# A written TensorE order of dense blocks in a decode kernel with all its gradients

## The chip, the cores and the metric

The kernel runs on one core of one Trainium2 chip. The metric is the device time of one execution in microseconds (us). Every time below is the median of several executions, with the lowest and highest beside it where they matter. An execution that came out over 1.5% above the fastest of its kernel is called slow and left out of ratios. A ratio is the mean time of one kernel's fast runs over the mean time of the other kernel's fast runs in the same rounds on the same chip, so it is not quite the ratio of the medians quoted. A median takes in the slow executions too, so differences are given of medians and, where it matters, of the means of the fast runs. The batches ran on different chips. The fast runs of the kernel before have means of 566 to 571 us in them, so a difference between batches is sure to some 5 us only.

## The reference, cut to what matters

```python
# B=2, Sq=1, D=576, Hq=32, Hkv=16, Sk=4096, Dh=128, F=4608, all bf16
def _fwd_reference(A_x, A_k_cache, A_v_cache, A_wq, A_wo, B_x, B_w_gate, B_w_up, B_w_down):
    x = A_x
    xn = _layernorm(x)
    # A: q = xn @ wq; scores against k_cache; softmax; times v_cache; @ wo   (decode: one token)
    # B: (xn @ w_gate) * (xn @ w_up) @ w_down
    return x + _A_ref(xn, ...) + _B_ref(xn, ...)

def reference(..., grad_out):
    _out, _vjp = jax.vjp(_f, A_x, A_k_cache, A_v_cache, A_wq, A_wo, B_w_gate, B_w_up, B_w_down)
    return (_out, *_vjp(grad_out))
```

So the kernel reads both caches and all weights once (92.48 MB) and writes gradients of the same size (92.48 MB). The gradients of the caches and of the weights are outer products: TensorE makes them in PSUM, ScalarE and VectorE copy them to SBUF ("evacuate"), and DMA stores them.

## The kernel before

The work goes in 16 iterations, one for two K/V heads of one batch row. An iteration has eight "half heads". For each, VectorE transposes half of a head into `X`, and TensorE makes 16 score matmuls from it:

```python
    def ps_sc(): return ps.tile([P, P], FP32, tag="sc", bufs=2, name="ps_sc")      # scores
    def ps_o():  return ps.tile([P, 2, 512], FP32, tag="o", bufs=2, name="ps_o")   # outer products: two buffers

    def head_scores(n, t, x, s_ps, half):
        X = xtile([P, NCH, 64], "X")                         # 3 buffers
        t32(view(pairs(X[:]...)), view(pairs(n[:]...)))      # VectorE transpose
        for e in range(2):
            be = 2 * half + e
            for c8 in range(8):
                nc.tensor.matmul(s_ps[:], lhsT=view(W[t][:], ...), rhs=view(X[:], ...), ...)
```

The gradient of a K or V head leaves in units. Each unit takes one `ps_o` buffer, four matmuls in two row quadrants, and one copy:

```python
        def unit(A, cp):
            def f():
                if cp == 0:
                    m["st"] = stile([P, 2, 2, 8, Dh], "so")          # store buffer
                o = ps_o()
                for k in range(2):
                    for aa in range(2):
                        a = 2 * A + aa
                        nc.tensor.matmul(view(o[:], ...), lhsT=rows[32 * a:32 * a + 32, 2 * cp + k, :],
                                         rhs=bd[32 * a:32 * a + 32, :], start=True, stop=True)
                evac(view(m["st"][:], ...), o[:]..., 1024)
                if cp == 3:
                    ...                                              # two DMA stores
```

The weights' gradients have units of the same kind. Their store buffers (`stw`, `std`, `stq`, `sto`) share one pool of two:

```python
    def swtile(shape, name):
        return sb.tile(list(shape), BF16, tag="sw", bufs=2, name=name)

        def outer_o(A, h2, k):      # output projection: one store buffer per A, filled by four units
            def f():
                if h2 == 0 and k == 0:
                    m["so"] = swtile([P, 4, D], "sto")
                ...
```

One thing the text of the kernel does not show: the order in which TensorE gets its instructions is not that of the text. A scheduler of the framework chooses it when the program is built, from what is ready in its own estimate, so score blocks, outer units, softmax steps and weight pieces are laid between one another in small pieces.

Of the kernel before, what the change touches and what calls it, by code (L numbers as in the profile page):

```python
# [23 lines left out]
def kernel(  # L24
# [55 lines left out]
    def ps_o():  # L80
        return ps.tile([P, 2, 512], FP32, tag="o", bufs=2, name="ps_o")

# [177 lines left out]
    def dxn(Wm, Wt, weight, pos, koff, kstep):  # L260


        for half in range(2):
            dp = ps_m([P, 160])
            X = xtile([P, 9, FS // 2], "Xw")
            t32(view(pairs(X[:].rearrange("p c n -> p (c n)")), 0, P, 0, [[1, 9 * P]]),
                view(pairs(weight[:].rearrange("p c n -> p (c n)")), 0, P, P * half, [[2 * P, 9], [1, P]]))
            dve(1.4)
            for r in range(4):
                for gq in range(4):  # L270
                    q, s = 2 * half + gq // 2, 4 * (gq % 2) + r
                    nc.tensor.matmul(  # L272
                        dp[32 * gq:32 * gq + 32, 0:P], lhsT=view(Wm[:], 0, P, 8 * pos(q, s), [[1, 32]]),
                        rhs=view(X[:], 0, P, koff(s) * 256 + (2 * (q % 2) + (s // 2) % 2) * 64 + s % 2,
                                 [[kstep * 256, 4], [2, 32]]),
                        start=(r == 0), stop=(r == 3))
            for r in range(2):
                for gq in range(4):
                    q, s = 2 * half + gq // 2, 2 * (gq % 2) + r
                    nc.tensor.matmul(  # L280
                        dp[32 * gq:32 * gq + 32, P:160], lhsT=view(Wt[:], 0, P, 8 * (4 * q + s), [[1, 32]]),
                        rhs=view(X[:], 0, P, 8 * 256 + (2 * (q % 2) + s // 2) * 64 + s % 2, [[2, 32]]),
                        start=(r == 0), stop=(r == 1))
            nc.vector.tensor_add(accx[:], accx[:], dp[:])
            dve(0.35)


    def mlp_units(i):
# [62 lines left out]
        def back():  # L351
            dxn(*m["W"], m["wgu"], lambda q, s: q * 8 + s, lambda s: (s // 4) * 4, 1)

        def outer_gu(w, A):
            def f():
                hb = m["hb"]
                if A == 0:
                    m["st"] = swtile([P, 4, FS], "stw")
                st = m["st"]
                o = ps_o()  # L360
                for dc in range(4):
                    for aa in range(2):
                        a = 2 * A + aa
                        nc.tensor.matmul(o[:, aa, dc * P:(dc + 1) * P],  # L364
                                         lhsT=xnr[32 * a:32 * a + 32, dc * P:(dc + 1) * P],
                                         rhs=hb[32 * a:32 * a + 32, 1 + w, :], start=True, stop=True)
                evac(view(st[:], 0, P, 256 * A, [[P, 2], [FS, 4], [1, P]]),
                     o[:].rearrange("p a (d f) -> p a d f", d=4), 1024)
                if A == 1:
                    out = (out_6, out_7)[w]  # L370
                    nc.gpsimd.dma_start(out[0:512, f0:f0 + FS].rearrange("(c p) n -> p c n", p=P), st[:])  # L371
            return f

        def outer_tail():
            hb = m["hb"]
            st = tailtile("stt")
            for A in range(2):
                o = ps_o()
                for w in range(2):
                    for aa in range(2):  # L380
                        a = 2 * A + aa
                        nc.tensor.matmul(o[64 * w:64 * w + 64, aa, 0:P], lhsT=xnr[32 * a:32 * a + 32, 512:576],
                                         rhs=hb[32 * a:32 * a + 32, 1 + w, :], start=True, stop=True)
                evac(st[:, 256 * A:256 * A + 256].rearrange("p (a f) -> p a f", a=2), o[:, :, 0:P], 256)
            for w, out in enumerate((out_6, out_7)):
                nc.gpsimd.dma_start(out[512:576, f0:f0 + FS], st[64 * w:64 * w + 64])

        def outer_down(A, k):
            def f():
                hb = m["hb"]  # L390
                if A == 0 and k == 0:
                    m["sd"] = swtile([P, FC, D], "std")
                st = m["sd"]
                o = ps_o()
                for aa in range(2):
                    a = 2 * A + aa
                    nc.tensor.matmul(o[:, aa, 0:HD2], lhsT=hb[32 * a:32 * a + 32, 0, :],  # L397
                                     rhs=dyr[32 * a:32 * a + 32, k * HD2:(k + 1) * HD2], start=True, stop=True)
                evac(st[:, 2 * A:2 * A + 2, k * HD2:(k + 1) * HD2], o[:, :, 0:HD2], D)
                if A == 1 and k == 1:  # L400
# [3 lines left out]
        return [[loads], [gate_up, down], [grads, back], [outer_down(0, 0), outer_down(0, 1)], [outer_down(1, 0), outer_down(1, 1)],  # L404
                [outer_gu(0, 0), outer_gu(0, 1)], [outer_gu(1, 0), outer_gu(1, 1)], [outer_tail]]
# [14 lines left out]
    def group_front(g, wq, wo):  # L420
        qd = sb.tile([P, 3, GH, 2], BF16, tag="qd", bufs=2, name="qd")
        qp = ps_m([P, GH, 2])
        for h in range(GH):
            for dc in range(5):
                if dc < 4:
                    l, r = wq[:, 2 * dc + h // 4, (h % 4) * P:(h % 4 + 1) * P], xs[:, dc, 0:2]
                else:
                    l, r = wq[:, 8, (h % 4) * P:(h % 4 + 1) * P], xs[:, 4 + h // 4, 0:2]
                nc.tensor.matmul(qp[:, h, :], lhsT=l, rhs=r, start=(dc == 0), stop=(dc == 4))
        nc.vector.tensor_copy(qd[:, 0], qp[:])  # L430
        nc.vector.tensor_scalar(qd[:, 2], qd[:, 0], SCALE, None, op0=ALU.mult)

        do_ps = ps_m([P, GH * 32])
        for half in range(2):
            Xo = xtile([P, GH // 2, D], "Xo")
            t32(pairs(Xo[:].rearrange("p c n -> p (c n)")),
                pairs(wo[:, 4 * half:4 * half + 4].rearrange("p c n -> p (c n)")))
            for k in range(NB):
                for e in range(2):
                    nc.tensor.matmul(  # L440
                        do_ps[:, P * half:P * half + P], lhsT=Wdy[:, k, e, :],
                        rhs=view(Xo[:], 0, P, 64 * k + e, [[D, 4], [2, 32]]),
                        start=(k == 0 and e == 0), stop=(k == NB - 1 and e == 1),
                    )
        dof = sb.tile([P, GH, 32], FP32, tag="dof", bufs=1, name="dof")
        t32(dof[:].rearrange("p c n -> p (c n)"), do_ps[:])
        nc.vector.tensor_copy(qd[:, 1], dof[:, :, 0:2])


        rp = ps_m([P, 2, 4, GH * 2])  # L450
        for t in range(2):
            for be in range(4):
                nc.tensor.matmul(rp[:, t, be, :], lhsT=sel[:, be].rearrange("p a i -> p (a i)"),
                                 rhs=qd[:, t].rearrange("p h b -> p (h b)"), start=True, stop=True)
        rep = sb.tile([P, 2, 4, GH * 2], BF16, tag="rep", bufs=2, name="rep")
        nc.vector.tensor_copy(rep[:], rp[:])
        dve(2.6 + 1.2)
        return dict(g=g, wq=wq, wo=wo, qd=qd, rep=rep, oT=oTs[g % 2])
# [50 lines left out]
    def contract(rowsT, heads):  # L509
# [13 lines left out]
        o_sb = sb.tile([P, Dh], FP32, tag="o_sb", bufs=1, name="o_sb")  # L523
        nc.scalar.copy(o_sb[:], o_ps[:])
        act(0.3)
        t_ps = ps_m([P, 4])
# [11 lines left out]
    def outer_units(rows, bd, b, l0, oview):  # L538
        m = {}

        def unit(A, cp):
            def f():
                if cp == 0:
                    m["st"] = stile([P, 2, 2, 8, Dh], "so")
                o = ps_o()
                for k in range(2):
                    for aa in range(2):
                        a = 2 * A + aa
                        nc.tensor.matmul(view(o[:], 0, P, 512 * aa + P * k, [[256, 2], [1, P]]),  # L549
                                         lhsT=rows[32 * a:32 * a + 32, 2 * cp + k, :],  # L550
                                         rhs=bd[32 * a:32 * a + 32, :], start=True, stop=True)
                evac(view(m["st"][:], 0, P, 2 * cp * Dh, [[8 * Dh, 4], [1, 2 * Dh]]),
                     o[:].rearrange("p a (x c) -> p (a x) c", x=2), 1024)
                if cp == 3:
                    for aa in range(2):
                        nc.gpsimd.dma_start(oview[b, 2 * A + aa, :, l0:l0 + 2],  # L556
                                            m["st"][:, aa].rearrange("p x c d -> p x (c d)"))
            return f
        return [unit(A, cp) for A in range(2) for cp in range(4)]

    def softmax(s_ps):
        mx = small("mx")
        nc.vector.reduce_max(mx[:], s_ps[:], axis=AX.X)
        mT = ps_m([1, P])
        nc.tensor.transpose(mT[:], mx[:], identf[:])
        m4 = small("m4", (1, 4))
# [307 lines left out]
```

## Time and profile before

| | before |
|---|---|
| median of 3 runs | 571.89 us (568.31 to 573.84) |
| profiled span, mean TensorE clock | 561.8 us, 0.802 |
| TensorE busy | 472.1 us, 84% of the span |
| transfers | 186.13 MB, 329 GB/s over the span |

The page and the waits that carry the argument are shown and read in the prediction. The timeline of TensorE has the columns: start us, us, engine, line, operation, output and inputs, shapes, count. The timeline of TensorE before the change has the columns: start us, us, engine, line, operation, output and inputs, shapes, count; in brackets the idle time just before and what ended it.

```profile
123.80 1.08 PE L503 MATMUL ps_sc<-X,W 128*128 128x128 bf16 x16
124.82 0.61 PE L549 MATMUL ps_o<-bd,dsm 32*128 32x256 bf16 x8
125.36 1.09 PE L503 MATMUL ps_sc<-X,W 128*128 128x128 bf16 x16
126.38 0.39 PE L549 MATMUL ps_o<-bd,dsm 32*128 32x256 bf16 x4
126.70 0.18 PE L340 MATMUL ps_m<-gT,selA 128*128 128x16 bf16 x1
127.23 0.39 PE L549 MATMUL ps_o<-bd,dsm 32*128 32x256 bf16 x4 [0.34 <-ACT so L93]
```

At 126.38 one half of an outer unit (4 matmuls) is issued; the next half must wait until ScalarE has emptied a `ps_o` buffer. A weight-gradient matmul (L340) is laid into that time, and 0.34 us of it stay idle.

### The profile page before, as it was taken

To read this page: it belongs to the slowest core of one execution; us is meant where nothing else is said; L and a number is where in the kernel's file an instruction comes from. 1 tells how busy PE (TensorE), PEld (TensorE's weight loads), DVE (VectorE), ACT (ScalarE), POOL (GpSimd) and SP (SyncE) were. 2 spreads that over 40 slices of the span, in tenths; PEclk is the share of its full clock that TensorE was granted. 3 is DMA by queue.
4 is the path that set the end of the run, shared out by engine and by line. 5 is a ranking of instruction groups with operands and counts; after the bars stand their busy time and mean duration, and the time that the engine had idled before them with its cause. 6 is when DMAs were issued, how large, how long until landed. Compare 5 with 4: busy or idle time off the path is not lost. (4 is left out here: it accounts for less than half of the span.)

```text
span 561.8 us, 18035 instructions
## 1 busy us (share of the span) xinstructions
PE 472.1 (84%) x7897; PEld 336.5 (60%) x7897; DVE 369.6 (66%) x637; ACT 343.6 (61%) x473; POOL 193.3 (34%) x404
## 2 busy tenths in 40 slices
PE   2688859998989799999888973999898999888842
PEld 1576637676766465676677752666676666666511
DVE  8696836747656545738577672685787567788336
ACT  1146856857666264657667662686767559778631
POOL 5222443422432233333423441263433324433231
PEclk9899987857885655558888995697999569999656
DMA  8996999999699599689997897799999979985471
GB/s 259 407 395 225 418 407 383 339 369 365 189 412 404 199 304 410 229 305 395 360 398 270 342 418 310 263 404 415 363 399 381 420 275 385 394 347 219 158 270 49
DMA packets 53927, 186.13 MB, mean 331 GB/s; under 512 B 5164, under 2 KB 20152, under 8 KB 45656
## 3 DMA queue, kind: packets, MB, share of 16 engines
q1 hardware_dynamic: 28392, 92.49, 44.1%
q0 software_dynamic: 25456, 92.48, 42.1%
q8 instruction: 62, 1.02, 0.7%
q14 instruction: 17, 0.14, 0.1%
HBM read 92.48 MB, written 92.48 MB: 329 GB/s over the span
## 5 line engine op out<-in xcount | busy, mean ns | idle before, releaser
L93 ACT CAST so<-ps_o 128x1024 bf16<-128x1024 f32 x240 | 231.9, 1023 | 93.9 <-PE ps_o L549 90.1
L503 PE MATMUL ps_sc<-X,W 128*128 128x128 bf16 x2048 | 185.8, 240 | 2.5 <-DVE X L102 2.4
L102 DVE STREAM_TRANSPOSE X<-kv 128x1024 f32<-128x1024 f32 x128 | 157.5, 1233 | 33.6 <-PE ps_sc L503 27.7
L503 PEld LDWEIGHTS <-W 128*128 128x128 bf16 x2048 | 144.0, 107 | 34.6 <-issue 28.7
L556 POOL DMA_DIRECT2D out_dram<-so x128 | 91.4, 716 | 169.7 <-ACT so L93 74.0
L549 PE MATMUL ps_o<-bd,prm 32*128 32x256 bf16 x512 | 52.9, 304 | 10.5 <-ACT stq L93 4.7
L549 PE MATMUL ps_o<-bd,dsm 32*128 32x256 bf16 x512 | 54.8, 302 | 6.8 <-ACT so L93 4.4
L518 PE MATMUL ps_m<-kv,rowT 128*32 128x128 bf16 x2048 | 56.3, 251 | 1.0 <-issue 0.9
L518 PEld LDWEIGHTS <-rowT 128*32 128x32 bf16 x2048 | 38.4, 110 | 17.2 <-issue 13.8
L93 ACT CAST stw<-ps_o 128x1024 bf16<-128x1024 f32 x32 | 31.4, 1023 | 15.6 <-PE ps_o L364 8.8
L467 POOL COPY W<-rep 32x16 bf16<-32x16 bf16 x128 | 30.7, 240 | 20.6 <-PE ps_sc L503 13.7
L549 PEld LDWEIGHTS <-prm 32*128 32x128 bf16 x512 | 21.4, 98 | 22.6 <-issue 11.1
L549 PEld LDWEIGHTS <-dsm 32*128 32x128 bf16 x512 | 21.3, 98 | 19.8 <-issue 10.8
L93 ACT CAST std<-ps_o 128x576 bf16<-128x576 f32 x36 | 23.0, 648 | 12.9 <-PE ps_o L397 12.6
L474 POOL COPY dM<-qd 128x128 bf16<-128x128 bf16 x32 | 9.1, 289 | 61.7 <-PE ps_m L480 38.2
L93 ACT CAST stq<-ps_o 128x1024 bf16<-128x1024 f32 x10 | 9.9, 1013 | 28.3 <-DMA out_dram<-sto 26.1
L102 DVE STREAM_TRANSPOSE Xw<-wgu 128x1152 f32<-128x1152 f32 x18 | 24.5, 1362 | 3.3 <-PE ps_sc L503 3.3
L90 DVE CAST so<-ps_o 128x1024 bf16<-128x1024 f32 x16 | 19.3, 1208 | 11.1 <-PE ps_o L549 10.3
L93 ACT CAST sto<-ps_o 128x576 bf16<-128x576 f32 x30 | 18.8, 641 | 12.5 <-PE ps_o L684 12.3
L722 DVE TENSOR_SCALAR oT<-ps_m 128x4 bf16<-128x4 f32 x16 | 2.7, 170 | 35.4 <-PE ps_m L527 35.4
L371 POOL DMA_DIRECT2D out_dram<-stw x18 | 13.6, 753 | 23.0 <-ACT stw L93 11.5
L533 DVE TENSOR_TENSOR dsm<-ds,maskc 128x1024 bf16<-128x1024 bf16 x16 | 19.0, 1186 | 0.0
(178 smaller groups left out, 586.5 us busy)
## 6 DMA issues: line engine op xcount, KB each, us to landing
out_dram<-so POOLq DMA_DIRECT2D x128, 512.0 KB, 8.9
kv<-in_A_k_cache_dram SPq DMA_DIRECT2D x32, 1024.0 KB, 10.3
kv<-in_A_v_cache_dram SPq DMA_DIRECT2D x32, 1024.0 KB, 10.3
out_dram<-stw POOLq DMA_DIRECT2D x18, 512.0 KB, 9.1
wd<-in_B_w_down_dram SPq DMA_DIRECT2D x9, 576.0 KB, 9.5
out_dram<-std POOLq DMA_DIRECT2D x9, 576.0 KB, 6.9
wo<-in_A_wo_dram SPq DMA_DIRECT2D x4, 1152.0 KB, 13.6
wgu<-in_B_w_gate_dram SPq DMA_DIRECT2D x9, 512.0 KB, 11.7
```

The lines of the kernel that those rows point to most:

```text
L90: nc.vector.tensor_copy(out=out, in_=in_)
L93: nc.scalar.copy(out, in_)
L102: nc.vector.transpose(out, in_)
L371: nc.gpsimd.dma_start(out[0:512, f0:f0 + FS].rearrange("(c p) n -> p c n", p=P), st[:])
L467: nc.gpsimd.tensor_copy(view(W[t][:], 32 * a, 32, 28 + 32 * a, [[2 * WW, 4], [WW + 2, 2], [1, 2]]), view(st["rep"][:], 32 * a, 32, t * 4 * ...
L474: nc.gpsimd.tensor_copy(view(dM[:], 0, P, t * 2 * P, [[P + 2, 2], [4, 32], [1, 2]]), view(st["qd"][:], 0, P, (2 if t == 0 else 1) * GH * 2 ...
L503: nc.tensor.matmul(s_ps[:], lhsT=view(W[t][:], 0, P, (be * 2 + x) * WW + 28 - 4 * c8, [[1, P]]), rhs=view(X[:], 0, P, c8 * 64 + e, [[8 * 6 ...
L518: nc.tensor.matmul(o_ps[32 * cg:32 * cg + 32, :], lhsT=view(rowsT[:], 0, P, c4 * 32 + 4 * c8, [[1, 32]]), rhs=head[:, 8 * c4 + c8, :], sta ...
L533: nc.vector.tensor_tensor(m[:], view(rows[:], 0, P, 0, [[0, 8], [1, P]]), view(maskc[:], 0, P, 0, [[1, 8], [0, P]]), ALU.mult)
L549: nc.tensor.matmul(view(o[:], 0, P, 512 * aa + P * k, [[256, 2], [1, P]]), lhsT=rows[32 * a:32 * a + 32, 2 * cp + k, :], rhs=bd[32 * a:32 ...
L556: nc.gpsimd.dma_start(oview[b, 2 * A + aa, :, l0:l0 + 2], m["st"][:, aa].rearrange("p x c d -> p x (c d)"))
L722: nc.vector.tensor_scalar(st["oT"][:, 1, 4 * s:4 * s + 4, b], t_ps[:], SCALE, None, op0=ALU.mult)
```

## The change

The intent is to cut the switches between kinds of matmul: a switch is a pair of neighbours on TensorE that use the array in different tile shapes, and the prediction reads its price from the trace (some 93 ns each at full clock, 135 at half). TensorE's order is fixed to that of the text, and the text is laid out anew so that each half head is: one block of 16 scores, one K/V outer unit of four row quadrants (two `ps_o` buffers), one link of the chain (softmax, contraction, projection), about one weight piece.

```diff
+    ctx.enter_context(tc.manual_schedule(engines={mybir.EngineType.PE}))
...
-        def unit(A, cp):
+        def unit(cp):
             def f():
                 if cp == 0:
-                    m["st"] = stile([P, 2, 2, 8, Dh], "so")
-                o = ps_o()
+                    m["st"] = [stile([P, 2, 2, 8, Dh], "so") for _ in range(2)]
+                o = [ps_o(), ps_o()]
                 for k in range(2):
-                    for aa in range(2):
-                        a = 2 * A + aa
-                        nc.tensor.matmul(view(o[:], ...), ...)
-                evac(view(m["st"][:], ...), o[:]..., 1024)
+                    for a in range(4):
+                        nc.tensor.matmul(view(o[a // 2][:], ...), ...)
+                for A in range(2):
+                    evac(view(m["st"][A][:], ...), o[A][:]..., 1024)
...                                                       # the weights' units in the same way
-        def outer_o(A, h2, k):
+        def outer_o(h2, k):
...
+                if h2 == 0 and k == 0:
+                    m["so"] = [stq([P, 4, D], "sto") for _ in range(2)]     # both store buffers at once
...
+    for n in range(NIT + 1):
+        ...
+        for j in range(8):
+            head_scores(heads[x], t, x, cur[("s_ps", "dp_ps")[t]], half)    # 16 scores
+            more()                                                          # one K/V outer unit
+            if prev:
+                ...                                  # j = 0..3: contraction, selection of the iteration before
+            if live:
+                if 4 <= j < 7:
+                    soft[j - 4]()                    # one step of the softmax
+                ...
+                other(-(-len(side) // (12 - j)))     # about one weight piece
```

The arithmetic and the bytes stay the same.

## The prediction

> **What bounds the kernel now.** I read the page's header and its slices first, then TensorE's rows by form, the table of windows, the waits of each engine, and last the chain that ended last. A "slot" below is a half head: one transpose of keys or values into X on VectorE and 16 score matmuls. There are 128 of them (16 iterations of 8), so 562 us are 4.4 us a slot.
>
> ```profile
> PE 472.1 (84%) x7897; PEld 336.5 (60%) x7897; DVE 369.6 (66%) x637; ACT 343.6 (61%) x473; POOL 193.3 (34%) x404
> PEclk9899987857885655558888995697999569999656
> DMA  8996999999699599689997897799999979985471
> HBM read 92.48 MB, written 92.48 MB: 329 GB/s over the span
> ```
>
> TensorE is the busiest, but look at the two rows of digits: where the granted clock falls to 5 or 6, the transfers fall to 5 to 7 tenths, and where the clock is 9 they are at 9. The same from the windows (columns: busy us and instructions of each engine, granted clock, DMA share, GB/s):
>
> ```profile
> 200.00:240.00 40.00, 38.76 (x514) 25.32 (x513) 22.21 (x38) 24.11 (x32) 12.40 (x25) 0.54 0.84 307
> 400.00:440.00 40.00, 36.20 (x752) 27.46 (x751) 28.85 (x50) 28.87 (x38) 14.75 (x35) 0.97 0.98 380
> 460.00:500.00 40.00, 36.52 (x644) 25.51 (x644) 31.84 (x49) 32.61 (x44) 18.20 (x40) 1.00 0.99 387
> 520.00:562.00 42.00, 21.02 (x284) 10.63 (x276) 18.61 (x33) 15.74 (x20) 10.29 (x16) 0.58 0.43 157
> ```
>
> At 200 to 240 TensorE is busy 97% of the time and issues 514 matmuls; at 400 to 440 it issues 752. With a half clock TensorE is the bound; with a full one the kernel moves 380 to 387 GB/s and the DMA engines are full. The waits agree that it is not loads that hold anything up: no entry has VectorE waiting for a K or V load. The evacuations wait for TensorE:
>
> ```profile
> ACT so L93 <- PE ps_o L549: 90.1, 79, 4.0
> ACT stq L93 <- DMA out_dram<-sto: 26.1, 4, 9.9
> DVE X L102 <- PE ps_sc L503: 27.7, 31, 2.9
> PEld L503 <- issue: 28.7, 113, 0.7
> PE ps_o L549 <- ACT so L93: 7.8, 27, 0.5
> ```
>
> ScalarE waits 90 us for outer products, TensorE only 8 us for ScalarE. The 28.7 us of "issue" ahead of score weights, 113 times, are the price of coming back to scores from another kind of matmul. A stretch at half clock shows it, and a dense block at full clock beside it:
>
> ```profile
> 200.63 0.61 PE L549 MATMUL ps_o<-bd,prm 32*128 32x256 bf16 x4
> 201.17 0.29 PE L503 MATMUL ps_sc<-X,W 128*128 128x128 bf16 x1
> 201.39 0.40 PE L549 MATMUL ps_o<-bd,prm 32*128 32x256 bf16 x2
> 505.53 1.08 PE L503 MATMUL ps_sc<-X,W 128*128 128x128 bf16 x16
> ```
>
> [...] From the start times of neighbouring matmuls at full clock: score to score 57 ns (median), score to a 32-row outer product 150 ns, outer product to score 200 ns where its own 256 columns would need about 107. So some 93 ns a switch; at half clock (107, 241, 350 ns) some 135. [...] The trace's clock records are 0.5 or 1.0 only, in multiples of 3.41 us. I weighed each matmul of a window with its columns times its share of the 128x128 array (4 concurrent 32-row tiles count as one): whether this exceeds 0.34 of what a full clock could stream tells the next window's clock in 151 of 157 cases. 93 windows had a full clock, 65 a half one. [...] the trace has 3 to 6 ns between two quadrants. [...]
>
> **The change part by part.** The program built from each version (its order of instructions, no times) has the same 7813 matmuls and nearly the same ScalarE and VectorE work: 239 of 256 K/V evacuations on ScalarE against 240. What differs:
>
> 1. TensorE's order. Score runs go from 253 (mean 8.1) to 128 of exactly 16; contractions from 89 runs to 32 of 64; K/V outer products from 198 runs (105 of them of 4) to 125 nearly all of 8. Mode switches fall from 736 to 446. 290 x 0.093 = 27 us at full clock, 290 x 0.135 = 39 us at half.
> 2. An outer unit uses four row quadrants, not two. 8 matmuls of 256 columns then need two streams of 107 ns, not four. Their seven gaps cost 5+5+5+107+5+5+5 = 137 ns, against 7 x 39 in the mean of before: 128 x 0.136 = 17 us, at half clock 128 x 0.243 = 31 us.
> 3. Adding all start-to-start gaps by kind of neighbours over both orders: before 347 us at full clock and 585 at half; after 305 and 518, less item 2 288 and 487. Before spent 0.396 of its time at half clock, so without waits it would need 1/(0.604/347 + 0.396/585) = 412 us; 562 - 412 = 150 us are waits, of whatever kind. The new order at the same clock: 344 us.
> 4. The clock. Array work is 207 us (columns times share, all matmuls). Over 562 us this is 0.37, hardly above 0.34: hence the flapping, and the stretch at 199 to 247 us that stays at half. [...] In the new order, run without waits at half clock, it is 207/487 = 0.43: it should recover. At 505 us the mean is 0.41. Each slot also has its 16 score matmuls (16 x 53 = 0.85 us of array work), which evens it out. I expect a mean of about 0.90, not 1.0.
> 5. PSUM. A unit now takes both ps_o buffers. TensorE may start the next one only as the two evacuations end. Chain of before, near the end, where this already happens:
>
> ```profile
> 534.31 1.02 ACT so L93
> 535.33 0.04 issue
> 535.37 0.43 PE ps_o L684 x2
> 535.81 0.02 issue
> 535.83 0.65 ACT sto L93
> ```
>
> ScalarE is idle 0.50 us for each such turn. 201 units (128 of K/V, 73 of weights) x 0.5 = 100 us, on 344 us of ScalarE work: 444 us if every turn were exposed. This costs, but stays below item 6.
> 6. Transfers. 186.13 MB unchanged; at the 387 GB/s of a full-clock stretch 481 us. The start (0 to 20 us at 300 GB/s) loses some 5 us. The end now moves 157 GB/s x 42 us = 6.6 MB, 17 us' worth, so it loses 25. The last group's stores get buffers of the large pool and the last layer norm is laid between them: I take 18 lost instead of 25, a guess.
>
> Sum: TensorE 344 + 150 of waits = 494 us if clock and waits stay; transfers 481 + 5 + 18 = 504. The larger stands: a span of 504 us, 506 with the 1.8 us by which the timed run (563.56) exceeded its span (561.8). That is 12% below 571.89. The three timed runs of before are 5 to 10 us over the profiled one, so before is uneven by itself.
>
> **The rivals.** First, a rigid order waits where the old one filled in. In the old order a score block could be interrupted by whatever was ready; now one late X tile, one late small matmul of the softmax or a late store buffer stops everything behind it. For it: the 26.1 us of stq waiting for a store, up to 9.9 us at a time, and TensorE idle 9.4 us at 344 us because of it; the new output-projection piece takes both small store buffers at once. Against: chain links are spread one to a slot, a slot (4 us) being longer than any step of them. With 60 us more of waits: 565 us, the same as before. Second, the ps_o turn of item 5 becomes the bound in weight-heavy iterations: 16 K/V and some 24 weight evacuations, 20 turns at 0.5 us, some 43 us against some 41 us of transfers there. Worth 10 to 20 us: 515 to 525. Third, the clock goes to 1.0 and stores flow evenly: 186.13 MB at the 415 GB/s of the best slices is 449 us; with start and end 475 to 480. Fourth, stores: K/V output tiles are now allocated and sent in pairs, 2 MB at a time, and have four slots to land (16 us) where they had six. The median landing is 8.9 us; with full queues this can stall ScalarE; 5 to 15 us.
>
> **Range and chances.** Third rival alone gives 478, second and fourth together 540: this is my range for 8 in 10. Within 2% of before (560 to 583) needs the first rival in full, slower more than that. Since the gaps by kind show 68 us of TensorE time removed in any clock, and no work is added: faster 0.88, same 0.08, slower 0.04.
>
> **What would show it.** Score groups in runs of 16; "issue" ahead of score weights about halved; TensorE busy well below 84% of a smaller span, or below 400 us; mean clock 0.88 or more; slices with 9 tenths DMA through the middle; ScalarE's 90 us wait for outer products at 50 to 100, and TensorE's wait for ScalarE up from 8 us to several tens. Wrong would be: a clock still near 0.80 (item 4), TensorE idle over 120 us on one kind of wait (first rival), or ScalarE busy plus its waits on ps_o filling the span while DMA stays below 8 tenths (item 5).

## The result, and the profile after

The changed kernel is slower: 648.29 us (642.67 to 656.20, 4 runs, one of them slow) against 572.87 us (568.31 to 578.96, 4 runs) for the kernel before; ratio 1.131, 95% interval 1.119 to 1.144. Both profiles are of fast runs. The same rows of the page as the prediction shows, now of the changed kernel:

```profile
PE 451.3 (70%) x7897; PEld 341.7 (53%) x7897; DVE 372.2 (58%) x649; ACT 345.2 (54%) x473; POOL 190.2 (30%) x404
PEclk9986677596665776579675866876676768787755
DMA  8967998488895889977997689984899388974474
HBM read 92.48 MB, written 92.48 MB: 289 GB/s over the span
```

The span is 640.9 us. TensorE is busy for less time (451.3 against 472.1 us) but only 70% of the span; no engine is over 70%. The stretches of half clock have not gone; the digits of the clock are lower nearly everywhere (mean 0.718 against 0.802). One line of the windows view for 300 to 500 us, first before, then after (busy us and instruction counts of PE, PEld, DVE, ACT and POOL; then clock, DMA share, GB/s):

```profile
300.00:500.00 200.00, 176.96 (x3055) 126.26 (x3056) 139.21 (x225) 135.92 (x187) 75.26 (x163) 0.87 0.92 361
```

```profile
300.00:500.00 200.00, 143.32 (x2492) 109.41 (x2490) 109.87 (x186) 110.98 (x151) 55.44 (x121) 0.70 0.86 314
```

TensorE, VectorE and ScalarE issue 17 to 19% fewer instructions in the same time, GpSimd 26%. That is what a kernel looks like whose engines wait for one another. The waits after (engine and line, what ended the wait, total us, times, longest us):

```profile
ACT so L95 <- PE ps_o L556: 150.4, 112, 7.3
ACT sto L95 <- DMA out_dram<-stw: 27.8, 3, 9.8
PE ps_o L556 <- ACT sto L95: 23.6, 3, 8.5
PEld L508 <- issue: 21.3, 39, 5.6
PE ps_o L394 <- ACT so L95: 17.0, 30, 1.0
PE ps_o L556 <- DVE prm L541: 14.4, 6, 3.0
PE ps_o L363 <- ACT so L95: 13.9, 20, 1.1
PE ps_o L705 <- ACT so L95: 13.5, 20, 1.0
DVE X L104 <- DMA kv<-in_A_v_cache_dram: 31.9, 8, 5.6
DVE X L104 <- DMA kv<-in_A_k_cache_dram: 11.2, 3, 7.7
```

Three readings. "issue" ahead of the score weights is down from 113 times to 39: the blocks are dense, as meant (its total fell less, from 28.7 to 21.3 us, as the longest now lasts 5.6 us). VectorE now waits 43.1 us for K and V tiles, where before it waited for none; TensorE in turn waits 9.1 us for `X` (run 8 looks at the loads). But the largest change is elsewhere: TensorE waited 12.7 us in all for copies into `so` before, at four lines (7.8 of it at L549), and now waits 60.2 us at six: mostly at L394, L363 and L705, which are weight pieces that stand right behind another outer unit and find both `ps_o` buffers full. And there are three waits of some 8 us each at L556. One of these three, in the timeline of TensorE:

```profile
339.70 1.05 PE L508 MATMUL ps_sc<-X,W 128*128 128x128 bf16 x8
340.68 0.39 PE L556 MATMUL ps_o<-bd,dsm 32*128 32x256 bf16 x2
349.21 0.61 PE L556 MATMUL ps_o<-bd,dsm 32*128 32x256 bf16 x6 [8.13 <-ACT sto L95]
350.72 0.42 PE L705 MATMUL ps_o<-dyr,R 32*128 32x288 bf16 x2 [0.89 <-ACT so L95]
351.64 0.42 PE L705 MATMUL ps_o<-dyr,R 32*128 32x288 bf16 x2 [0.49 <-ACT so L95]
```

The outer unit has issued two matmuls of its eight and stands 8.13 us for the other `ps_o` buffer. VectorE's timeline beside it, and the chain of waits of the same stretch (start us, us, what):

```profile
335.99 1.25 DVE L104 STREAM_TRANSPOSE X<-kv 128x1024 f32<-128x1024 f32 x1 [1.16 <-PE ps_sc L508]
340.79 1.38 DVE L104 STREAM_TRANSPOSE Xw<-wq 128x1152 f32<-128x1152 f32 x1 [2.93 <-PE ps_sc L508]
349.90 0.16 DVE L585 TENSOR_SCALAR negb<-ps_m 128x1 f32<-128x1 f32 x1 [7.73 <-PE ps_m L583]
```

```profile
332.53 15.89 DMA out_dram<-stw
348.42 0.02 issue
348.44 0.04 ACTq L95
348.48 0.04 issue
348.52 0.65 ACT sto L95
349.17 0.04 issue
349.21 0.43 PE ps_o L556 x3
```

Read it backwards. The outer unit needs a `ps_o` buffer; the copy that empties it goes into `sto`; that store buffer is still held by an earlier gradient slice (`stw`), whose store takes 15.89 us. The `X` that VectorE finished at 337.24 belongs to the next score block, as counting transposes and blocks in the trace shows; that block starts at 352.59, 15 us later, because it stands behind the unit. VectorE then stands for 7.73 us as well. In the trace three weight loads and two matmuls of the unit were issued before this stop, and in the 8.13 us no matmul of any kind started.

I added up all such standing time from the trace: wherever two matmuls that follow each other on TensorE start more than 450 ns apart, the excess over 250 ns. Before the change it is 66.7 us in 87 gaps; after, 175.5 us in 181. The difference, 109 us, is more than the 79 us by which the span grew.

### The profile page after: what moved, and what is told of

Same layout as the page of the kernel before. It is cut to its first block, busy times and chain, and to the rows that moved or that the text cites. A ratio compares the mean times of both kernels' runs of the same rounds, so it can differ in the third digit from the quotient of the medians.

```text
span 640.9 us, 18016 instructions
## 1 busy us (share of the span) xinstructions
PE 451.3 (70%) x7897; PEld 341.7 (53%) x7897; DVE 372.2 (58%) x649; ACT 345.2 (54%) x473; POOL 190.2 (30%) x404
## 4 chain that ended last, share of the span: by engine, by line
PE 32%; ACT 13%; DMA 10%; DVE 8%; issue 7%; POOL 1%; POOLq 0%; SPq 0%; ACTq 0%; DVEq 0%
PE ps_sc L508 13%; ACT so L95 10%; DMA out_dram<-stw 7%; PE ps_o L556 6%; PE ps_m L523 4%; DVE X L104 3%; DMA out_dram<-sto 2%; DVE so L92 2%; PE ps_m L442 1%; DMA wq<-in_A_wq_dram 1%; ACT stw L95 1%; PE ps_m L274 1%; PE ps_o L363 1%; POOL out_dram L564 1%; PE ps_o L394 1%
## 5 line engine op out<-in xcount | busy, mean ns | idle before, releaser
L508 PE MATMUL ps_sc<-X,W 128*128 128x128 bf16 x2048 | 190.2, 262 | 12.1 <-DVE X L104 9.1
L508 PEld LDWEIGHTS <-W 128*128 128x128 bf16 x2048 | 164.5, 118 | 26.3 <-issue 21.3
L556 PE MATMUL ps_o<-bd,dsm 32*128 32x256 bf16 x512 | 38.5, 334 | 32.8 <-ACT sto L95 23.6
L556 PE MATMUL ps_o<-bd,prm 32*128 32x256 bf16 x512 | 38.3, 344 | 19.9 <-DVE prm L541 14.4
L523 PE MATMUL ps_m<-kv,rowT 128*32 128x128 bf16 x2048 | 48.6, 269 | 0.3 <-issue 0.3
L556 PEld LDWEIGHTS <-dsm 32*128 32x128 bf16 x512 | 10.7, 98 | 46.9 <-issue 43.0
L556 PEld LDWEIGHTS <-prm 32*128 32x128 bf16 x512 | 10.5, 99 | 33.1 <-DVE prm L541 15.5
L394 PE MATMUL ps_o<-dyr,hb 32*128 32x288 bf16 x72 | 14.0, 392 | 17.5 <-ACT so L95 17.0
L363 PE MATMUL ps_o<-hb,xnr 32*128 32x128 bf16 x288 | 12.3, 252 | 17.5 <-ACT so L95 13.9
L257 POOL COPY Wt<-Wm 64x128 bf16<-64x128 bf16 x26 | 7.5, 288 | 54.2 <-DVE Wm L251 48.7
```

The source lines that it names most:

```text
L363: nc.tensor.matmul(o[a // 2][:, a % 2, dc * P:(dc + 1) * P], lhsT=xnr[32 * a:32 * a + 32, dc * P:(dc + 1) * P], rhs=hb[32 * a:32 * a + 32, ...
L394: nc.tensor.matmul(o[a // 2][:, a % 2, 0:HD2], lhsT=hb[32 * a:32 * a + 32, 0, :], rhs=dyr[32 * a:32 * a + 32, k * HD2:(k + 1) * HD2], star ...
L508: nc.tensor.matmul(s_ps[:], lhsT=view(W[t][:], 0, P, (be * 2 + x) * WW + 28 - 4 * c8, [[1, P]]), rhs=view(X[:], 0, P, c8 * 64 + e, [[8 * 6 ...
L523: nc.tensor.matmul(o_ps[32 * cg:32 * cg + 32, :], lhsT=view(rowsT[:], 0, P, c4 * 32 + 4 * c8, [[1, 32]]), rhs=head[:, 8 * c4 + c8, :], sta ...
L556: nc.tensor.matmul(view(o[a // 2][:], 0, P, 512 * (a % 2) + P * k, [[256, 2], [1, P]]), lhsT=rows[32 * a:32 * a + 32, 2 * cp + k, :], rhs= ...
```

## The experiments

The theories. **A**: the fixed order is the cost; each wait stops all that stands behind it (the prediction's first rival). **B**: the units of two `ps_o` buffers are the cost (the second rival). **C**: what the new layout does to loads, stores and the softmax chain, whatever the order on TensorE. **D**: the lower clock is itself the cause. Each kernel is an edit of the changed kernel unless said otherwise. All gave correct results. Fifteen ran, in four batches. Where an expectation speaks of C, it means the layout with its loads and stores.

### 1. The order given back to the scheduler (e1_auto)

```diff
-    ctx.enter_context(tc.manual_schedule(engines={mybir.EngineType.PE}))
```

> The changed kernel with TensorE's order left to the scheduler again (four-quadrant units, unit lists, store buffers all kept); its built order has 794 mode switches, where the written order has 446 and before 736. Theory A (the fixed written order is what waits: it cannot fill a hole with other work): 575 to 600 us, most of the loss back. Theory B (four-quadrant units take both ps_o buffers, whoever orders them, so evacuation and matmul no longer overlap): stays at 630 us or more. Theory C (loads and stores: K/V heads held one iteration longer, both small store buffers taken at once): also stays above 620 us.

Measured: 598.92 us (588.30 to 603.62), before at 572.35. Three of the four executions count as slow against the fastest, so no ratio was given. The fast one, the profiled one, is 58 us below the fast mean of the changed kernel (646.4) and 18 above that of the kernel before (570.2); by medians it is 49 and 27 of 76 us. All this comes off with one line, though the built order now has 794 switches in place of 446. From the profile:

```profile
PE 461.6 (79%) x7897; PEld 325.3 (55%) x7897; DVE 367.9 (63%) x649; ACT 343.0 (58%) x473; POOL 190.7 (33%) x404
PEclk9889959569695868989967958959887669869865
PE ps_o L704 <- ACT sto L94: 19.1, 5, 11.0
```

Gaps over 450 ns fall from 175.5 to 100.0 us, and TensorE's waits for copies into `so` from 60.2 to 12.2 us, where they were before the change. The waits for `sto` stay. The clock is 0.804 in this execution and 0.762 in the three slow ones, against 0.684 to 0.718 with the written order. A holds for the larger part, with a time inside its range; some 18 to 27 us stay.

One caution: taking the line out changes more than TensorE's order. By the two traces, 96 of VectorE's 649 instructions, 29 of ScalarE's 473 and 63 of GpSimd's 404 leave the order that both kernels share. No run holds the other engines' orders still, so "the fixed order" means here also what the build makes of it on the others.

### 2 and 3. Units of one buffer (e2_halves, e3_halves_auto)

```diff
-                o = [ps_o(), ps_o()]
-                for k in range(2):
-                    for a in range(4):
-                        nc.tensor.matmul(view(o[a // 2][:], ...), ...)
                 for A in range(2):
+                    o = ps_o()
+                    for k in range(2):
+                        for a in (2 * A, 2 * A + 1):
+                            nc.tensor.matmul(view(o[:], ...), ...)
                     evac(...)
```

This is in all outer units; the second kernel also gives the order to the scheduler.

> The changed kernel with its written order, but each outer unit made as two halves, one ps_o buffer and two quadrants each, so that one half is evacuated while the other is computed; still 446 mode switches. Theory A (fixed order): hardly faster than the changed kernel, 625 to 650 us. Theory B (both ps_o buffers at once): the some 75 us of TensorE gaps ahead of outer units that ended with an evacuation shrink to a third, 575 to 600 us. Theory C: 625 us or more.

> Both undone: units in halves and TensorE's order left to the scheduler; what remains of the change is the unit lists, their pacing, the stores in pairs and the K/V heads held one iteration longer. Theories A and B both expect about the time of before, 565 to 590 us. Theory C expects 600 us or more, the rest of the loss still there.

Measured: 642.48 us (633.85 to 643.85), ratio 1.122 (1.110 to 1.134), in the written order; 596.30 us (592.21 to 603.72), ratio 1.046 (1.032 to 1.059), under the scheduler. By medians the two-buffer units are worth some 6 us in the one and 3 in the other. By fast runs it is 7 us in the one, with intervals that overlap, and in the other the halves are 7 us slower (594.9 against the single 588.3), so neither is clear of the noise. B falls as the main cause. The second kernel came out between what A and B expected (565 to 590) and what C expected (600 or more). The gaps stay at 162.7 us in the written order; my reading is that two halves one behind the other still fill both buffers, and what comes right behind still waits.

### 4. The kernel before with its own text order fixed (e4_before_manual)

```diff
# of the kernel before
+    ctx.enter_context(tc.manual_schedule(engines={mybir.EngineType.PE}))
```

> The kernel before with TensorE bound to the order in which its own source is written (402 mode switches, score runs of 16, contraction runs of 64), everything else as it was: its softmax links stand one behind the other. Theory A (a fixed order waits): slower than before by over 8%, 620 us or more. Theory B: near before or faster through fewer switches, 540 to 580 us, as its units use one ps_o buffer each. Theory C: near before, 560 to 590 us.

Measured: 704.13 us (700.84 to 708.53), ratio 1.235 (1.225 to 1.246), clock 0.664, with only 402 switches in place of 736. Its waits:

```profile
ACT so L95 <- PE ps_o L551: 184.7, 107, 7.3
PE ps_m L573 <- DVE mr L571: 24.0, 16, 2.5
PE ps_m L529 <- ACT o_sb L526: 15.1, 31, 1.0
```

TensorE stands once in each of the 16 iterations for the softmax's maximum (L573) and 31 times for the copy inside the contraction (L529). In the changed kernel the first of these is a single wait of 1.2 us and the second is absent at its own place (4.6 us for that copy are left at two weight pieces): laying the chain out over the slots took these away. So the written order is a good one as fixed orders go (648 against 704 us), and fewer switches than before came with a slower kernel both times.

### 5 to 7. Mending the written order (e5_split, e6_store_order, e7_both)

The fixed order stays. First, the score block is cut so that no two outer units are neighbours:

```diff
# cut to what moves
-                head_scores(heads[x], t, x, ..., half)          # 16 scores
-                more()                                          # K/V outer unit
-                ...                                             # chain link
-                other(...)                                      # weight piece
+                head_scores(X, t, x, ..., half, 0)              # 8 scores
+                more()
+                ...
+                head_scores(X, t, x, ..., half, 1)              # 8 scores
+                other(...)
```

> The changed kernel, still in its written order, with each block of sixteen score matmuls cut in two of eight: the K/V outer unit and the chain link stand between the two eights, the weight piece after the second, so that no two units that fill the outer-product buffers stand next to each other. Theory A1 (what the fixed order loses is mostly the wait of one outer or weight unit for the evacuation of the unit just ahead of it, some 75 us of the 175 us of gaps): 600 to 620 us, with the waits of outer units for the copies out of their buffers falling from some 75 us to under 30 us. Theory A2 (the fixed order loses at many places, each wait for a late input or buffer stopping everything behind it, so spreading one kind moves the loss on): 630 to 655 us.

Measured: 631.60 us (630.91 to 633.62); before at 577.29, with only one fast execution of seven (566.24), so no ratio. It takes off some 14 us by fast runs, 17 by medians. That is inside what A2 expected, at its lower end, and not what A1 expected. The waits of the weight pieces for copies into `so` fell (L394 from 17.0 to 3.2 us, L363 from 13.9 to 8.4, L705, now L706, from 13.5 to 2.8). But part of the loss moved, as A2 says: the K/V units now wait 13.2 us for copies into `stw` (3.0 before), and twelve of them came too early for their masked probabilities and waited 20.3 us, in place of six and 14.4 us.

Second, the output-projection units take one store buffer, fill it, send it, then take the other:

```diff
-        def outer_o(h2, k):
...
-                    m["so"] = [stq([P, 4, D], "sto") for _ in range(2)]
-                o = [ps_o(), ps_o()]
+        def outer_o(A, h2):
...
+                if h2 == 0:
+                    m["so"] = stq([P, 4, D], "sto")
+                for k in range(2):
+                    o = ps_o()
...
```

The edit also makes these units take one `ps_o` buffer at a time, as run 2 does in all units; the two are not tested apart here.

> The changed kernel with the output-projection outer units reordered so that they need one of the two store buffers at a time instead of both at once. If the three stops of 7 to 9 us each, where TensorE waits for a store to free the second buffer, are lost time: 615 to 628 us and those stops gone (-20 to -30 us). If those stops only take slack that the queue of loads and stores would have asked for elsewhere: 640 to 650 us, with as much waiting in other places.

Measured: 620.30 us (617.30 to 624.47): 28 us less (26 by fast runs), as expected if the stops were lost time. The three waits behind `sto` are gone; what is left of ScalarE's own is this:

```profile
ACT sto L95 <- DMA out_dram<-stw: 6.0, 2, 3.1
```

The gaps fell by 28 us, 24 of them these three stops, and the time fell by about as much. Third, these two and the halves of run 2 together:

> The changed kernel in its written order with halves (one buffer per unit), the split score blocks and the reordered output-projection units together. If the losses add: 560 to 590 us, at or near the kernel before. If the fixed order itself is the cost (theory A2): 610 to 640 us, still above the 599 us that the unmended change took under the scheduler.

Measured: 597.16 us (595.97 to 600.64). The three single gains, 5.8 + 16.7 + 28.0 = 50.5 us, predict 597.8; by fast runs 6.8 + 14.5 + 25.8 predict 599.3 and 597.7 came. The losses add (the output-projection units are in halves in both run 2 and run 6, so a little is counted twice). My expectation for that case (560 to 590) was too low, because I had hoped for more from the split. Gaps are down to 110.0 us. The line for 300 to 500 us:

```profile
300.00:500.00 200.00, 166.83 (x2865) 121.37 (x2858) 126.52 (x209) 125.71 (x172) 64.97 (x139) 0.70 0.93 344
```

### 8. Later loads (e8_auto_late_loads)

```diff
# under the scheduler, as in run 1
-            if n % 4 == 2 and g + 1 < NGRP:              # weights of the next group
+            if n % 4 == 3 and g + 1 < NGRP:
...
-                if j == 3 and n in (0, 1, 2, 4, 6, 8, 10, 12):
+                if j == 7 and n in (0, 1, 2, 4, 6, 8, 10, 12):
```

> The changed kernel with TensorE's order left to the scheduler (599 us before this edit), the group's weight loads asked for one iteration later and the slice's loads four half heads later, so that they hold the shared load buffers for a shorter time. Theory C (the 25 us that remain over the kernel before are K and V tiles that come late because early-asked weights hold their buffers): 570 to 585 us, and VectorE's waits for K and V tiles fall from some 40 us to under 20. If the remainder is the order of stores and copies instead: 592 to 605 us.

Measured: 604.23 us (600.21 to 606.31, all fast), no gain over run 1. VectorE's waits for K and V tiles did fall, from 48.6 us (V 41.3, K 7.3) to 26.7 us (V 2.5, K 24.2), and it bought nothing. What remained was in the stores:

```profile
PE ps_o L704 <- ACT sto L94: 30.4, 5, 10.8
ACT sto L94 <- DMA out_dram<-stw: 29.5, 3, 10.9
```

So 22 us fewer of these waits bought nothing: a wait that a table shows need not be felt at the end of the kernel. That the loads cost nothing at all is not shown, since the K tiles came later than in run 1.

### 9 to 11. More array work on purpose (e9_before_warm, e10_after_warm, e11_both_warm)

```diff
-                s_ps[:], lhsT=..., rhs=view(X[:], 0, P, c8 * 64 + e, [[8 * 64, 4], [2, 32]]),
+                s_ps[:, 0:(2 if c8 in (0, 7) else 1) * P], lhsT=...,
+                rhs=view(X[:], 0, P, c8 * 64 + e, [[0, 2 if c8 in (0, 7) else 1], [8 * 64, 4], [2, 32]]),
```

This is the edit cut to the matmul; the buffer is made twice as wide, and its readers take the first half. Four of every sixteen score matmuls stream their columns twice, into a half of the buffer that nobody reads.

> The kernel before with four of every sixteen score matmuls streaming their 128 columns twice into a part of the buffer that nobody reads: 512 matmuls get 128 columns more, some 27 us of array work at the full clock on top of 207 us. If array work per 3.41 us window sets the next window's clock [...]: mean clock from 0.80 to 0.85 or more. The time: if the low clock is itself a cost of this kernel, 545 to 570 us in spite of the added work; if loads and stores or waits set it, 572 to 590 us.

> The same edit on the changed kernel in its written order. If array work sets the clock: from 0.718 to 0.79 or more. If the low clock is a cause of the lost time (theory D): 600 to 630 us. If the clock only follows from the waits, which stay (theory A): 635 to 660 us, the added 27 us of streaming about paid by the higher clock and the waits as before.

> The same edit on the mended version (halves, split score blocks, one store buffer at a time; 597 us, clock 0.702, the lowest clock for its speed [...]). If evenness just under the threshold is what holds it at 597 us: clock over 0.80 and 555 to 580 us. If waits hold it: 595 to 610 us.

Measured: 582.76 us for the kernel before so edited (ratio 1.022, 1.014 to 1.030; clock 0.81); 648.67 us for the changed one (641.09 to 655.41, ratio 1.128; clock 0.81); 603.78 us for the mended one (595.42 to 607.72, ratio 1.048). Its two fast runs have a mean of 597.9 us at clocks of 0.79, run 7 one of 597.7 at 0.70 to 0.72, which is what waits, not evenness just under the 0.34 of the prediction, would give. The changed kernel is the telling case:

```profile
PE 441.6 (69%) x7897; PEld 323.3 (51%) x7897; DVE 371.7 (58%) x649; ACT 345.1 (54%) x473; POOL 189.4 (30%) x404
PEclk9886977988875788879985878879996757789855
PE ps_o L556 <- ACT sto L95: 30.7, 3, 10.7
```

The clock rose from 0.718 to 0.81 with the added array work (some 27 us, an estimate: 512 x 53 ns): windows of 3.41 us at full clock went from 74 of 180 to 110 of 181. The time did not move, and the gaps did not either (181.1 us against 175.5). This test has a limit. From the prediction's item 3, the changed order needs 288 us at full clock and 487 at half; with 512 matmuls of 128 columns more, 315 and 541 (53 and 107 ns each: 107 is the step of score matmuls measured at half clock, 53 half of it). At a clock of 0.81, that is 0.38 of the time at half, TensorE without waits needs 1/(0.62/315 + 0.38/541) = 374 us; at 0.718 (0.564 at half) without the edit it also needs 374. So the added work used up what the clock gave. What the run shows is that the waits of the changed kernel, 640.9 - 374 = 267 us, stay at 639.2 - 374 = 265 when the clock rises by 13%: they are not made of slow matmuls. Both figures are estimates from item 3. In the kernel before the clock hardly rose (0.802 to 0.810), and I expected 0.85 or more there: a miss. D is thus not settled, but nothing here speaks for it as the main cause.

### 12 to 15. The mends under the scheduler (e12_both_auto, e13_store_auto, e14_split_auto, e15_both2_auto)

Each is one of the kernels above without the line that fixes the order: all three mends; the store order alone; the split alone. The last is all three with two weight pieces (the back projection) ahead of the output-projection units:

```diff
-        return [output, turn, spread, outer_o(0, 0), outer_o(0, 1), back(0), back(1), outer_o(1, 0), ...
+        return [output, turn, spread, back(0), back(1), outer_o(0, 0), outer_o(0, 1), outer_o(1, 0), ...
```

> The mended version (halves, split score blocks, one store buffer at a time) with TensorE's order left to the scheduler. If what the three mends remove and what the scheduler removes are different losses: 565 to 585 us, as fast as the kernel before. If they remove the same waits in two ways: 592 to 605 us.

> The changed kernel with only the store-order mend (one of the two store buffers at a time) and TensorE's order left to the scheduler. Without the mend it took 599 us, with all three mends 567. If the pair of store buffers is a loss that the scheduler cannot fill, it carries most of the 32 us: 568 to 582 us. If the scheduler already filled those waits: 592 to 602 us.

> The changed kernel with only the split of the score blocks into eights and TensorE's order left to the scheduler (599 us without). If the split carries the 32 us between 599 and 567: 568 to 582 us. If spacing the outer units is something the scheduler does itself: 592 to 602 us.

> All three mends under the scheduler (567 us) with the two back-projection units put ahead of the output-projection outer units, so that the first of their store buffers is asked for later; three waits of 5 to 7 us for that buffer are left. If they are lost time: 545 to 560 us, and the waits of TensorE behind the copies into that buffer fall from 17 us to under 8. If not: 562 to 572 us.

Measured: all three mends 566.63 us (559.95 to 570.31), ratio 0.986 (0.971 to 1.001); store order alone 579.67 us (570.62 to 584.22), ratio 1.006 (0.990 to 1.022); split alone 598.45 us (595.86 to 601.63), ratio 1.050 (1.039 to 1.060); the last one 574.51 us (568.99 to 580.15, 6 runs), ratio 1.005 (0.994 to 1.015). So the split gains nothing under the scheduler, as I expected if the scheduler spaces the units itself. The pair of store buffers is what this scheduler did not fill around, and their mend alone brings 599 to 580 us by medians (588.3 to 573.7 by fast runs, the first of them a single one). Compare also runs 7 and 12, which differ in the one line that fixes the order: 597.7 against 562.3 us by fast runs. So the fixed order still costs some 35 us when all three mends are in. A line of the waits of run 12 shows that it still has stops at the store buffers, and the windows line that from 300 to 500 us it issues hardly more matmuls than run 7 (2883 against 2865, with 3055 before), at a higher clock; it makes its gain earlier (3179 against 2716 from 100 to 300 us):

```profile
PE ps_o L557 <- ACT sto L94: 16.8, 3, 7.0
```

```profile
300.00:500.00 200.00, 173.30 (x2883) 120.20 (x2884) 130.44 (x220) 127.42 (x175) 69.81 (x151) 0.79 0.92 345
```

The last kernel takes that wait down to 5.8 us and is no faster (574.5 against 566.6 us, in different batches). Neither of my two expectations (545 to 560, 562 to 572) held: with most of the stop gone, something else sets the pace there, and I did not find what.

All kernels in one table. Figures from slow profiles are left out; span, clock and gaps are of the profiled run alone.

| kernel | TensorE's order | median us | mean of fast runs, us | span us | clock | gaps over 450 ns, us |
|---|---|---|---|---|---|---|
| before | scheduler | 572 | 566 to 571 (all batches) | 561.8 | 0.802 | 66.7 |
| changed | written | 648.3 | 646.4 (3 of 4) | 640.9 | 0.718 | 175.5 |
| 1 | scheduler | 598.9 | 588.3 (1 of 4) | 586.5 | 0.804 | 100.0 |
| 2 halves | written | 642.5 | 639.6 (3 of 4) | 640.2 | 0.698 | 162.7 |
| 3 halves | scheduler | 596.3 | 594.9 (3 of 4) | 590.6 | 0.780 | 96.9 |
| 4 before | written | 704.1 | 704.4 (4 of 4) | 699.7 | 0.664 | 166.5 |
| 5 split | written | 631.6 | 631.9 (4 of 4) | 630.0 | 0.689 | 144.1 |
| 6 store order | written | 620.3 | 620.6 (4 of 4) | 619.8 | 0.707 | 147.6 |
| 7 all three mends | written | 597.2 | 597.7 (4 of 4) | 598.9 | 0.702 | 110.0 |
| 8 later loads | scheduler | 604.2 | 603.7 (4 of 4) | 600.4 | 0.792 | 108.7 |
| 9 before, wider scores | scheduler | 582.8 | 583.0 (4 of 4) | 582.4 | 0.810 | 65.6 |
| 10 wider scores | written | 648.7 | 643.1 (2 of 4) | 639.2 | 0.810 | 181.1 |
| 11 mends, wider scores | written | 603.8 | 597.9 (2 of 4) | - | - | - |
| 12 all three mends | scheduler | 566.6 | 562.3 (2 of 4) | 558.2 | 0.804 | 76.0 |
| 13 store order | scheduler | 579.7 | 573.7 (2 of 4) | - | - | - |
| 14 split | scheduler | 598.5 | 598.6 (4 of 4) | 599.9 | 0.749 | 85.8 |
| 15 mends, moved pieces | scheduler | 574.5 | 573.5 (5 of 6) | 573.9 | 0.756 | 75.1 |

The gap count is a good first guide, not the whole time: runs 12 and 15 have the same gaps, 16 us of span between them and different clocks.

## Why the prediction was wrong

It said 506 us, from the transfers of item 6, which stood just above TensorE's 494, and gave 4% to what happened. Point by point.

- **Items 1 and 2, switches and quadrants: not contradicted, but not seen alone.** The score blocks come in 128 runs of 16, and the step inside a block is still 57 ns at full clock. The evidence for less time in TensorE's own flow is indirect: span minus gaps over 450 ns is 495 us before and 465 us after, in spite of a lower clock.
- **The sum, "TensorE 344 + 150 of waits", is the step that failed.** The 150 us were carried over "of whatever kind" as if they belonged to the work. They belonged to the old order, which filled. Worked in the same way at the clock that was measured, TensorE needs 374 us without waits and the span is 640.9: the waits are 267 us, and TensorE's term stands far above the transfers. In steps: 561.8 - 68 (items 1 and 2 at the old clock) + 30 (374 in place of 344, the clock) + 117 (waits) = 641. This is an estimate, but the 109 us by which the gaps over 450 ns grew are measured, and run 1 takes 75 us of gaps and 49 to 58 us of time off by giving the order back.
- **The first rival was named and weighed too lightly.** It had 60 us more of waits as its full size; 117 came. The argument against it, that chain links are spread one to a slot, held for most of the chain: of the softmax waits of run 4 only 1.2 us are left, with 14.4 us for late masked probabilities. But the waits came at store buffers (26 to 28 us by run 6), which the rival had named ("takes both small store buffers at once", with 9.4 us of such a wait from before, which I did not multiply), and at outer units standing next to one another (14 to 17 us by run 5), which it had not. Nor would its sign have found it: no one kind of wait on TensorE is over 120 us, the loss is spread over many, the largest being the 60.2 us for copies into `so`.
- **Item 4, the clock: wrong in sign.** I expected 0.90 on an order "run without waits". With waits the same 207 us of array work are spread over 641 us, 0.32 of the time in place of 0.37, under the 0.34 that the prediction had read from the trace of before (151 of 157 windows). In the trace of the changed kernel 0.34 tells the next window's clock in 168 of 179 cases, 0.345 in 173 (in 148 of 157 before); the plain busy share of TensorE tells at best 146 of the 179. So the share of array work goes with the clock in both traces, which does not show what sets it; what failed is the 0.43 that I had put in. Run 1 shows the clock back at 0.762 to 0.804 when most of these waits go. That the clock is a cause of its own, and how much of its 30 us would stay if it were held full at no cost, no run shows: run 10 pays for its clock.
- **Item 5, the turn of `ps_o`: "costs, but stays below item 6" is right of the pair itself** (6 to 7 us by run 2, not clear of the noise), and wrong in where it looked. It counted ScalarE's idle time; the cost came on TensorE, 60 us of waits for `so` copies, where it had 13.
- **Item 6, transfers as the bound: never reached.** 289 GB/s over the span. The tail did not shrink either: from the last score matmul to the end it is 44 us after and 45 before.
- **The fourth rival had the right place, store buffers, at the wrong engine.** It saw ScalarE stalled by K/V stores for 5 to 15 us. It was the weights' store buffers, 26 to 28 us, and through `ps_o` all of TensorE.
- **Readings and sums that do not hold as written.** The two rows of digits do not go together as the prediction says: of 14 slices with a clock digit of 5 or 6, five have a DMA digit of 9 and one of 8. Item 3's first quotient gives 414, not 412 us, with the figures shown. "68 us removed in any clock" is the value for the mix of before; the same figures give 59 at full clock and 98 at half, of which items 1 and 2 explain 44 and 70. None of these would have turned the forecast.

Some 18 to 27 us of the 76 remained without the fixed order (run 1). With the store order mended the kernel is within the noise of the kernel before (run 13, ratio 0.990 to 1.022), and with the halves and the split as well it is no slower (run 12). Which of these two helps there, when neither gains alone (runs 3 and 14), stays open; so does what sets the time of run 15. No version is clearly ahead of the kernel before: the best, run 12, has an interval that reaches 1.0006.

## What to carry to other kernels

A wait is a property of an order, not of the work: when an engine's order is fixed, count again every wait that the old order filled, and expect each to stop all that stands behind it, as the one of 8.13 us did here. Before fixing an order, look for resources that two neighbours share (PSUM buffers, store buffers) and ask what the unit behind them would do if the slowest store seen in the trace came just then. If an order is to be fixed all the same, put work that needs no such buffer between units that do, and take store buffers one at a time.
